# A late routing table moved to PSUM, and an order on ScalarE in a 128-row expert unit

## The chip, the cores and the metric

The kernel runs on one core of a Trainium2 chip. The metric is device time in microseconds (us) of one execution. The kernel before takes 699.88 us, the median of three runs (699.31 to 701.46). The profile is of another execution, which took 696.43 us.

## The reference

Inputs are q, k, v of shape (8 batches, 8 heads, 576 positions, 64). Two attentions are added: a local one, in which a position sees the positions at most 3 away, and a coarse one over means of 4 positions, repeated 4 times. The sum, as 4608 tokens of 512 values, goes into a mixture of 8 experts. Each token goes to one expert:

```
logits = x @ w_gate + modality_bias[modality_id]
e_idx = np.argmax(logits, axis=1)
gate_w = probs[np.arange(N), e_idx]           # softmax of the logits, at the chosen expert
...
h = np.maximum(x[mask] @ w1[e], 0.0)          # 512 -> 1024
out[mask] = gate_w[mask, None] * (h @ w2[e])  # 1024 -> 512
```

All is fp32. The kernel splits each fp32 operand of an expert's matmul into a high and a low part and makes three matmuls of one (high by high, high by low, low by high).

## The kernel before

**Stages.** For about the first 270 us the kernel computes attention, the router's logits and the places of the tokens. After that come the experts: 11 units of rows, one after another. A unit has up to 512 rows of one expert (H = 4 blocks of 128 rows). The order (line 1190) is: two early units of 4 blocks, six more units of 4 blocks ("p", pairs), and then the late units ("m"): one of 2 blocks, one of a single block of 128 rows, and one of 2 blocks. Behind them a loop (L1254) takes what is left; its count comes from the routing.

**Tables.** Which expert and which rows a unit has is worked out on VectorE (DVE) by `table` (L665): a prefix sum over experts, then for each unit a one-hot row (`oh`), and products and sums with it. Three large scratch arrays are used: `m`, `oh` and `o2`. `pairs` (L747) makes the table of the "p" units. `late` (L759) makes that of the "m" units and of the loop, from values that `pairs` leaves; `rest` (L776) makes the loop's list out of it. In both, the scratch has the tag "o" in the pool `xp`, three buffers of 128x512 fp32. The output tiles `o` of the units (L989) use the same three buffers, and so do the ReLU results of the 128-row unit (L954). An output tile is free when its scatter to memory (L998, an indirect DMA that GpSimd, POOL, issues) has landed. `C.ltri` is a 128x16x16 triangle of ones that `table` multiplies with in its first step. `pairs` is called before unit 0, `late` before unit 1.

**A unit.** `compute` (L921): the first layer makes groups of 128x512 in PSUM (L939; PSUM tag "S", three banks). ScalarE (ACT) takes the ReLU into `hh` (L943) and DVE the low part into `hl` (L944); then the bank is free. `second` (L972) makes the second layer (L987); ACT scales the result by the gate into `o` (L990), and POOL scatters it. The rows of the next unit are transposed on TensorE (PE) meanwhile (`xsplit`, L912; PSUM tag "T", three banks), and split by ACT (`xh`, L915) and DVE (`xl`, L917).

**The 128-row unit.** `compute_half` (L948) turns the roles round: the rows are stationary and the weights stream. So its result has to be transposed. For each half g of the 1024 hidden values: 12 matmuls (L961), ReLU on ACT into an `o` tile (L963), four transposes on PE into `ht` (L966, tag "T"), a copy on ACT into `hh` (L968), and a subtraction on DVE into `hl` (L969).

**Weights.** A unit has eight chunks of 128x1024 fp32: four of W1, four of W2. `step` (L1219) loads and splits the next chunk; it runs one unit ahead (LEAD = 8). Each chunk is a load into one of four `raw` buffers (L827 for W1, L829 for W2, issued on SyncE's queue SP), a copy on ACT into the high part `whi` (L848), and a subtraction on DVE into the low part `wlo` (L854). Where a chunk goes into the tile `X`, its parts are called `whl`. Within the 128-row unit, `compute_half` itself calls `step` four times (W1 of the last unit), and `second` four times (W2 of the last unit).

**Order.** From the experts on nothing is ordered by hand except by `issue_after(x)`: an instruction traced inside it comes behind x in the queue of its engine, without a semaphore. A scheduler orders the rest as the program is built, by readiness and program order. On the chip each of ACT, DVE, POOL and SP takes its instructions strictly in that order: one that waits holds up those behind it.

Of the kernel before, what the change touches and what calls it, by code (L numbers as in the profile page):

```python
# [7 lines left out]
F32 = mybir.dt.float32  # L8
F32R = mybir.dt.float32r
BF16 = mybir.dt.bfloat16  # L10
I32 = mybir.dt.int32
AF = mybir.ActivationFunctionType
# [6 lines left out]
NTOK, DM, NE, DF = 4608, 512, 8, 1024  # L19
# [23 lines left out]
NUMAX = NFULL + 1 + NLOOP  # L43
# [3 lines left out]
TB, SB = 3, 3  # L47
# [24 lines left out]
def whole(pieces):  # L72

    while True:
        try:
            next(pieces)
        except StopIteration as x:
            return x.value
# [417 lines left out]
class Router:  # L496
# [165 lines left out]
        s.nc.vector.tensor_copy(n, ni)  # L662
        yield

    def table(s, n, base, U, nm, pool, tag, unit=256):  # L665


        nc, C, tp = s.nc, s.C, s.tp
        N = n.shape[1]
        m = (pool.tile([128, DM], F32, name=tag, bufs=3)[:, : N * N].rearrange("p (a b) -> p a b", a=N) if tag else  # L670
             tp.tile([128, N, N], F32, name=nm + "m"))
        incl = tp.tile([128, N], F32, name=nm + "incl")
        nc.vector.tensor_tensor(m, C.ltri[:, :N, :N], n.unsqueeze(1).broadcast_to([128, N, N]), op=ALU.mult)
        yield
        nc.vector.tensor_reduce(incl, m, op=ALU.add, axis=AX.X)
        yield
        excl = tp.tile([128, N], F32, name=nm + "excl")
        nc.vector.tensor_tensor(excl, incl, n, op=ALU.subtract)
        yield

        off = tp.tile([128, N], F32, name=nm + "off")
        nc.vector.scalar_tensor_tensor(off, excl, -float(unit), base, op0=ALU.mult, op1=ALU.add)
        yield
        sh = [128, U, N]
        ub = C.uf[:, :U].unsqueeze(2).broadcast_to(sh)
        if tag:
            oh, o2 = (pool.tile([128, DM], F32, name=tag, bufs=3)[:, : U * N].rearrange("p (u l) -> p u l", l=N)
                      for _ in range(2))
        else:
            oh, o2 = (tp.tile(sh, F32, name=nm + x) for x in ("oh", "o2"))  # L690
        nc.vector.tensor_tensor(oh, incl.unsqueeze(1).broadcast_to(sh), ub, op=ALU.is_gt)
        yield
        nc.vector.tensor_tensor(o2, excl.unsqueeze(1).broadcast_to(sh), ub, op=ALU.is_gt)
        yield
        nc.vector.tensor_tensor(oh, oh, o2, op=ALU.subtract)
        yield
        r = tp.tile([128, 2, U], F32, name=nm + "r")
        for i, qv in enumerate((off, C.e2[:, :N])):
            nc.vector.tensor_tensor(o2, oh, qv.unsqueeze(1).broadcast_to(sh), op=ALU.mult)
            yield  # L700
            nc.vector.tensor_reduce(r[:, i], o2, op=ALU.add, axis=AX.X)
            yield
        nc.vector.scalar_tensor_tensor(r[:, 0], C.uf[:, :U], float(unit), r[:, 0], op0=ALU.mult, op1=ALU.add)
        yield

        no = tp.tile([128, U], F32, name=nm + "no")
        nc.vector.tensor_scalar(no, C.uf[:, :U], incl[:, N - 1 : N], float(NSLOT), op0=ALU.is_ge, op1=ALU.mult)
        yield
        nc.vector.tensor_tensor(r[:, 0], r[:, 0], no, op=ALU.add)
        yield  # L710
        return r, incl, excl
# [47 lines left out]
    def late(s, c, pool):  # L759

        nc, tp = s.nc, s.tp
        d = whole(s.taken(s.pn, s.pexcl, NPAIR, "p"))
        nc.vector.tensor_tensor(d, d, s.d, op=ALU.add)
        nc.vector.tensor_scalar(d, d, 2.0, None, op0=ALU.mult)
        n = tp.tile([128, 2 * NE], F32, name="mn")
        base = tp.tile([128, 2 * NE], F32, name="mbase")
        whole(s.units_of(c, 127, n[:, :NE], "m"))
        whole(s.units_of(c, 255, n[:, NE:], "mh"))
        nc.vector.tensor_tensor(n[:, NE:], n[:, NE:], n[:, :NE], op=ALU.subtract)
        for i, x in enumerate((d, n[:, :NE])):  # L770
            nc.vector.scalar_tensor_tensor(base[:, NE * i : NE * i + NE], x, 256.0, s.C.ecap, op0=ALU.mult, op1=ALU.add)
        nc.vector.tensor_tensor(n[:, :NE], n[:, :NE], d, op=ALU.subtract)
        s.r, s.incl, _ = whole(s.table(n, base, NUMAX, "m", pool, "o"))
        return whole(s.index(s.r, NFULL + 1, "m"))

    def rest(s):  # L776
# [16 lines left out]
class Moe:  # L793
    def __init__(s, tc, ctx, C, psum, xs, tab, w1, w2, out):
        s.tc, s.nc, s.C, s.ps = tc, tc.nc, C, psum
        s.xs, s.tab, s.w1, s.w2, s.out = xs, tab, w1, w2, out
        s.wr = ctx.enter_context(tc.tile_pool(name="mwr", bufs=4))
        s.wa = ctx.enter_context(tc.tile_pool(name="mwa", bufs=1))
        s.xa = ctx.enter_context(tc.tile_pool(name="mxa", bufs=1))
        s.na, s.ne = 2, 4  # L800
        s.turn = {}
        s.nw = 12
        s.cw, s.after = 0, ()

    def open_early(s, ctx):

# [26 lines left out]
    def wsplit(s, raw, which):  # L833
        nc = s.nc
        i = s.cw % s.nw
        turn = s.cw = s.cw + 1
        if i < s.nw - 2:
            pool = s.wa if i < s.na else s.we if i < s.na + s.ne else s.wb
            hi = pool.tile([128, 1024], F32R, name=f"whi{i}")
            lo = pool.tile([128, 1024], F32R, name=f"wlo{i}")  # L840
        else:
            X = s.xg.tile([128, 2560], F32R, name="whl", tag="X")
            hi, lo = X[:, :1024], X[:, 1024:2048]
        with ExitStack() as order:
            if HOLD <= turn <= NHOLD and s.after:
                for x in s.after:
                    order.enter_context(s.tc.issue_after(x.ins))
            (nc.gpsimd.tensor_copy if turn <= 4 else nc.scalar.copy)(hi, raw)  # L848
        yield
        with ExitStack() as order:  # L850
            if HOLD <= turn <= NHOLD and s.after:
                for x in s.after:
                    order.enter_context(s.tc.issue_after(x.ins))
            (nc.gpsimd if turn == 4 else nc.vector).tensor_tensor(lo, raw, hi.bitcast(F32), op=ALU.subtract)  # L854
        if which == 0:
            return hi, lo
        return hi.rearrange("p (f d) -> p f d", f=2), lo.rearrange("p (f d) -> p f d", f=2)
# [90 lines left out]
    def compute_half(s, T, W, X, step, mid, J):  # L948

        nc = s.nc  # L950
        xh, xl = X
        hh, hl = s.hidden()
        for g in range(2):
            r = s.xp.tile([128, 512], F32, name="o", bufs=3)  # L954
            p = s.ps.tile([128, 512], F32, name="l1", tag="S", bufs=SB)
            for k in range(4):
                if k % 2 == 0:
                    step()
                wh, wl = W[k]
                for i, (a, x) in enumerate(((xh, wh), (xl, wh), (xh, wl))):  # L960
                    nc.tensor.matmul(p, a[:, k, 0:128], x[:, 512 * g : 512 * g + 512], start=(k == 0 and i == 0),  # L961
                                     stop=(k == 3 and i == 2))
            nc.scalar.activation(r, p, AF.Relu)  # L963
            p = s.ps.tile([128, 4, 128], F32, name="ht", tag="T", bufs=TB)
            for f in range(4):
                nc.tensor.transpose(p[:, f, :], r[:, 128 * f : 128 * f + 128], s.C.ident)  # L966
            h4 = hh[:, 4 * g : 4 * g + 4, 0:128]
            nc.scalar.copy(h4, p)  # L968
            nc.vector.tensor_tensor(hl[:, 4 * g : 4 * g + 4, 0:128], p, h4.bitcast(F32), op=ALU.subtract)  # L969
        s.second(T, W, hh, hl, 1, step, mid, J)  # L970

    def second(s, T, W, hh, hl, H, step, mid, J=None, last=0):  # L972
# [34 lines left out]
def build(tc, q, k, v, mid, w_gate, bias, w1, w2, out):  # L1007
    nc = tc.nc
    with ExitStack() as ctx:
# [3 lines left out]
        ps = ctx.enter_context(tc.tile_pool(name="ps", bufs=2, space=PSUM))  # L1013
        xs = dp.tile([NTOK + 1, DM], F32, name="xs")
        tab = dp.tile([NSLOT + CAP, 2], I32, name="tab")
        C = Consts(tc, cp, ps)
        moe = Moe(tc, ctx, C, ps, xs, tab, w1, w2, out)
        with ExitStack() as actx:
            ectx = ExitStack()
            ro = Router(tc, ctx, C, ps, xs, tab, tables)  # L1020
# [14 lines left out]
            N = 4 * B  # L1035
# [195 lines left out]
        for i, (_, _, H) in enumerate(order):  # L1231
            if i == 0:
                with tc.high_priority():
                    lists["p"] = ro.pairs(cnt, moe.xp)
            if i == 1:
                lists["m"] = ro.late(cnt, moe.xp)
            if i:
                gather(i + 2)

            def mid(h):  # L1240
                if i == h == 0:
                    gather(2)
                split(i + 1, h)

            if H == 1:
                moe.compute_half(Ts[i], Ws[i], Xs[i], step, mid, Js.get(i))
            else:
                moe.compute(Ts[i], Ws[i], Xs[i], H, step, mid, Js.get(i), i == N - 1)
# [45 lines left out]
```

## Time and profile before

| | |
|---|---|
| time of the profiled execution | 696.43 us |
| its span | 694.7 us |
| busy, share of the span: PE / DVE / ACT / POOL | 94% / 57% / 52% / 40% |
| mean DMA rate over the span | 154 GB/s |
| weight copies on ACT, L848 into `whi` | 70 of 1051 ns |
| weight subtractions on DVE, L854 into `wlo` | 73 of 1223 ns |

A timeline row has the start in us from the span's start, the length in us, the engine, the line of the kernel, the operation, output <- input, their shapes, and the count of merged instructions. In brackets stand the idle time of the engine ahead of it, and what ended it, as semaphores let it be inferred. A row of the windows view has the window and its length, then the busy time and count of PE, of PE's weight loads (PEld), DVE, ACT and POOL, then the granted PE clock (PEclk, 1.00 is full speed), the DMA share, and GB/s. Matmuls overlap, so a matmul's length is more than the distance to the next one.

### The profile page before, as it was taken

To read this page: it belongs to the slowest core of one execution; us is meant where nothing else is said; L and a number is where in the kernel's file an instruction comes from. 1 tells how busy PE (TensorE), PEld (TensorE's weight loads), DVE (VectorE), ACT (ScalarE), POOL (GpSimd) and SP (SyncE) were. 2 spreads that over 40 slices of the span, in tenths; PEclk is the share of its full clock that TensorE was granted. 3 is DMA by queue.
4 is the path that set the end of the run, shared out by engine and by line. 5 is a ranking of instruction groups with operands and counts; after the bars stand their busy time and mean duration, and the time that the engine had idled before them with its cause. 6 is when DMAs were issued, how large, how long until landed. Compare 5 with 4: busy or idle time off the path is not lost. (4 is left out here: it accounts for less than half of the span.)

```text
span 694.7 us, 16603 instructions
## 1 busy us (share of the span) xinstructions
PE 650.9 (94%) x6123; PEld 514.1 (74%) x6123; DVE 393.9 (57%) x867; ACT 362.5 (52%) x804; POOL 280.2 (40%) x366
## 2 busy tenths in 40 slices
PE   7899989988989889998999999999999999999896
PEld 4566666665657567886888888888888888889694
DVE  6778778898887977647445234333453243416610
ACT  4788888875887645443344324333344244425610
POOL 5777676866788692361210400303104011210211
PEclk9999999998999999999999999999999999999999
DMA  9899879998599959296652544607434355245600
GB/s 189 170 181 175 164 164 200 174 172 175 113 202 172 165 153 247 61 320 210 170 194 70 148 147 123 239 9 201 158 97 139 98 145 174 65 134 181 203 29 30
DMA packets 176421, 106.97 MB, mean 154 GB/s; under 512 B 136300, under 2 KB 154770, under 8 KB 176338
## 3 DMA queue, kind: packets, MB, share of 16 engines
q1 hardware_dynamic: 169138, 86.71, 54.1%
q0 software_dynamic: 7200, 19.18, 8.4%
q8 instruction: 49, 0.80, 0.6%
q14 instruction: 34, 0.28, 0.2%
HBM read 86.61 MB, written 19.51 MB: 153 GB/s over the span
## 5 line engine op out<-in xcount | busy, mean ns | idle before, releaser
L998 POOL DMA_INDIRECT out_dram<-o,tg x34 | 36.9, 1085 | 249.0 <-ACT o L990 194.0
L854 DVE TENSOR_TENSOR wlo<-raw,whi 128x1024 fp32r<-128x1024 f32 x73 | 87.5, 1223 | 80.0 <-ACT whi L848 75.4
L944 DVE SCALAR_TENSOR_TENSOR hl<-l,hh 128x512 fp32r<-128x512 f32 x72 | 49.3, 688 | 103.6 <-ACT hh L943 103.6
L987 PE MATMUL l<-whi,hh 128*128 128x512 f32 x256 | 100.4, 396 | 3.1 <-ACT hh L968 3.1
L987 PE MATMUL l<-whi,hl 128*128 128x512 f32 x256 | 100.0, 391 | 0.0
L987 PE MATMUL l<-wlo,hh 128*128 128x512 f32 x256 | 100.0, 391 | 0.0
L943 ACT ACTIVATE hh<-l 128x512 fp32r<-128x512 f32 x72 | 42.6, 596 | 108.9 <-PE l L939 108.9
L939 PE MATMUL l<-xh,whi 128*128 128x512 f32 (+1 forms) x256 | 95.3, 375 | 3.3 <-DVE rcnt L789 1.7
L939 PE MATMUL l<-xl,whi 128*128 128x512 f32 (+1 forms) x256 | 94.9, 371 | 0.0
L939 PE MATMUL l<-xh,wlo 128*128 128x512 f32 (+1 forms) x256 | 94.8, 370 | 0.0
L848 ACT CAST whi<-raw 128x1024 fp32r<-128x1024 f32 x70 | 71.4, 1051 | 32.7 <-DMA raw<-in_moe_w_dram 20.3
L990 ACT ACTIVATE o<-l,tg 128x512 f32<-128x512 f32 x37 | 25.3, 687 | 98.9 <-PE l L987 70.9
L987 PEld LDWEIGHTS l<-whi,hh 128*128 128x128 f32 x256 | 48.3, 189 | 12.9 <-ACT hh L968 3.4
L939 PEld LDWEIGHTS l<-xh,whi 128*128 128x128 f32 x256 | 48.1, 189 | 12.9 <-DVE hl L944 2.1
L987 PEld LDWEIGHTS l<-wlo,hh 128*128 128x128 f32 x256 | 48.2, 188 | 10.1
L987 PEld LDWEIGHTS l<-whi,hl 128*128 128x128 f32 x256 | 48.4, 189 | 9.5
L939 PEld LDWEIGHTS l<-xh,wlo 128*128 128x128 f32 x256 | 48.3, 189 | 8.3
L939 PEld LDWEIGHTS l<-xl,whi 128*128 128x128 f32 x256 | 48.3, 189 | 8.0
L636 POOL DMA_INDIRECT tab<-ig,si x36 | 38.4, 1066 | 37.7 <-DVE si L607 16.3
L479 PE MATMUL avl<-Pw,vw 128*64 128x96 f32 x768 | 47.8, 263 | 1.0 <-ACT Od L469 0.5
L479 PEld LDWEIGHTS avl<-Pw,vw 128*64 128x64 f32 x768 | 35.9, 143 | 14.2 <-issue 6.8
L917 DVE TENSOR_TENSOR xl<-xt,xh 128x512 fp32r<-128x512 f32 x37 | 24.3, 681 | 37.8 <-ACT xh L915 37.7
(254 smaller groups left out, 1314.0 us busy)
## 6 DMA issues: line engine op xcount, KB each, us to landing
raw<-in_moe_w_dram SPq DMA_DIRECT2D x176, 128.0 KB
raw<-in_moe_w_dram SPq DMA_DIRECT2D x44, 512.0 KB
vw<-in_v_dram SPq DMA_DIRECT2D x53, 180.0 KB
qt<-in_q_dram SPq DMA_DIRECT2D x30, 288.0 KB
kt<-in_k_dram SPq DMA_DIRECT2D x30, 288.0 KB
xs<-R SPq DMA_DIRECT2D x64, 128.0 KB
vw<-in_v_dram SPq DMA_DIRECT2D x15, 90.0 KB
xs<-R SPq DMA_DIRECT2D x12, 64.0 KB
```

The lines of the kernel that those rows point to most:

```text
L479: s.nc.tensor.matmul(p[64 * a : 64 * a + 64, c], vw[:, NB * (4 * (hp // 2) + hp % 2 + 2 * a) + k, :], Pw[:, 2 * k + a], start=True, stop=T ...
L636: i = nc.gpsimd.indirect_dma_start(out=s.tab[:, :], out_offset=bass.IndirectOffsetOnAxis(ap=C.si[:, t : t + 1], axis=0), in_=C.ig[:, t, :] ...
L848: (nc.gpsimd.tensor_copy if turn <= 4 else nc.scalar.copy)(hi, raw)
L854: (nc.gpsimd if turn == 4 else nc.vector).tensor_tensor(lo, raw, hi.bitcast(F32), op=ALU.subtract)
L917: nc.vector.tensor_tensor(xl[:, :, hs], p, xh[:, :, hs].bitcast(F32), op=ALU.subtract)
L939: nc.tensor.matmul(p[:, f % n, :], a[:, fs], x[:, k, :N], start=(k == 0 and i == 0), stop=(k == 3 and i == 2))
L943: nc.scalar.activation(hh[:, g, :N], p, AF.Relu)
L944: nc.vector.scalar_tensor_tensor(hl[:, g, :N], p, 0.0, hh[:, g, :N].bitcast(F32), op0=ALU.max, op1=ALU.subtract)
L987: nc.tensor.matmul(p, a[:, f, hs], x[:, f % 2, :], start=(f == 0 and i == 0), stop=(f == 7 and i == 2))
L990: nc.scalar.mul(o, p, T[:, h, 1:2].bitcast(F32))
L998: nc.gpsimd.indirect_dma_start(out=s.out[:, :], out_offset=bass.IndirectOffsetOnAxis(ap=T[:, h, 0:1], axis=0), in_=o, in_offset=None, boun ...
```

## The change

There are two edits.

The first concerns `late`. Its table no longer takes its scratch from the "o" buffers. `m` and `o2` are taken from the PSUM tag "T", the ring of the transposes (its three banks, TB = 3, stay three). `oh`, which holds only zeros and ones, is written as bf16 over the memory of `C.ltri`, which no later table reads. The table of `pairs` stays in the "o" buffers.

The second concerns the 128-row unit. `compute_half` leaves a list behind its second half: nothing, that half's ReLU, that half's copy into `hh`, and the copy once more. The next four weight copies (the W2 chunks of the last unit) take one entry each, and come behind it on ACT's queue.

```
-    def table(s, n, base, U, nm, pool, tag, unit=256):
+    def table(s, n, base, U, nm, pool, tag, unit=256, last=0):
...
-        m = (pool.tile([128, DM], F32, name=tag, bufs=3)[:, : N * N].rearrange("p (a b) -> p a b", a=N) if tag else
+        m = (pool.tile([128, DM], F32, name=tag, bufs=TB)[:, : N * N].rearrange("p (a b) -> p a b", a=N) if tag else
...
-        if tag:
-            oh, o2 = (pool.tile([128, DM], F32, name=tag, bufs=3)[:, : U * N].rearrange("p (u l) -> p u l", l=N)
+        if last:
+            oh = C.ltri.bitcast(BF16).rearrange("p a b -> p (a b)")[:, : U * N].rearrange("p (u l) -> p u l", l=N)
+            o2 = pool.tile([128, DM], F32, name=tag, bufs=TB)[:, : U * N].rearrange("p (u l) -> p u l", l=N)
+        elif tag:
+            oh, o2 = (pool.tile([128, DM], F32, name=tag, bufs=TB)[:, : U * N].rearrange("p (u l) -> p u l", l=N)
...
-        s.r, s.incl, _ = whole(s.table(n, base, NUMAX, "m", pool, "o"))
+        s.r, s.incl, _ = whole(s.table(n, base, NUMAX, "m", pool, "T", last=1))
...
-        s.cw, s.after = 0, ()
+        s.cw, s.after, s.before = 0, (), []
...
+            x = s.before.pop(0) if s.before else None
+            if x is not None:
+                order.enter_context(s.tc.issue_after(x.ins))
             (nc.gpsimd.tensor_copy if turn <= 4 else nc.scalar.copy)(hi, raw)
...
-            nc.scalar.activation(r, p, AF.Relu)
+            relu = nc.scalar.activation(r, p, AF.Relu)
...
-            nc.scalar.copy(h4, p)
+            copy = nc.scalar.copy(h4, p)
...
+        s.before = [None, relu, copy, copy]
         s.second(T, W, hh, hl, 1, step, mid, J)
...
-                lists["m"] = ro.late(cnt, moe.xp)
+                lists["m"] = ro.late(cnt, ps)
```

## The prediction

> **What bounds the kernel now.** I read the busy shares first, then the waits of TensorE (PE), then the timelines of the engines around those waits.
>
> ```profile
> PE 650.9 (94%) x6123; PEld 514.1 (74%) x6123; DVE 393.9 (57%) x867; ACT 362.5 (52%) x804; POOL 280.2 (40%) x366
> ```
>
> PE is busy for 94% of the span, and no other engine comes near. So the question is where PE stands still in the part of the program that the change touches, the expert stage. The list of PE's waits from 270 us to the end (total us, times, longest) has three entries:
>
> ```profile
> PE l L987 <- ACT hh L968: 3.1, 1, 3.1
> PE l L939 <- DVE rcnt L789: 1.7, 1, 1.7
> PE l L939 <- DVE hl L944: 0.9, 1, 0.9
> ```
>
> The two edits stand beside these three: the first beside the table of the late units, which is on VectorE (DVE) when the 1.7 and 0.9 us arise; the second beside the unit of 128 rows, whose `hh` copy is the 3.1 us. Outside them PE has always work, so time taken out of them comes off the span, if nothing else is late next.
>
> **The 128-row unit, as it is.** Timelines of ScalarE (ACT) and of PE (start, length):
>
> ```profile
> 651.57 1.05 ACT L848 CAST whi<-raw 128x1024 fp32r<-128x1024 f32 x1 [0.34 <-DMA raw<-in_moe_w_dram]
> 652.85 1.04 ACT L848 CAST whi<-raw 128x1024 fp32r<-128x1024 f32 x1 [0.23 <-DMA raw<-in_moe_w_dram]
> 655.03 1.04 ACT L848 CAST whi<-raw 128x1024 fp32r<-128x1024 f32 x1 [1.14 <-SPq L1254]
> 655.98 0.58 ACT L968 CAST hh<-ht 128x512 fp32r<-128x512 f32 x1
> 656.46 0.60 ACT L963 ACTIVATE o<-l 128x512 f32<-128x512 f32 x1
> 656.95 1.05 ACT L848 CAST whi<-raw 128x1024 fp32r<-128x1024 f32 x1
> 658.19 0.59 ACT L968 CAST hh<-ht 128x512 fp32r<-128x512 f32 x1 [0.20 <-PE ht L966]
> ```
> ```profile
> 652.63 0.39 PE L961 MATMUL l<-wlo,xh 128*128 128x512 f32 x1
> 652.86 0.60 PE L966 MATMUL ht<-ident,o 128*128 128x128 f32 x4
> 656.61 0.50 PE L987 MATMUL l<-whi,hh 128*128 128x512 f32 x1 [3.15 <-ACT hh L968]
> 657.11 1.04 PE L966 MATMUL ht<-ident,o 128*128 128x128 f32 x4
> 657.95 1.92 PE L912 MATMUL xt<-ident,xg 128*128 128x128 f32 x8
> 659.51 0.78 PE L987 MATMUL l<-whi,hl 128*128 128x512 f32 x1
> 660.51 0.47 PE L987 MATMUL l<-whi,hh 128*128 128x512 f32 x1
> ```
>
> The first transposes `ht` end at 653.46 (652.86 + 0.60). Their copy L968 starts only at 655.98: between stand the second and third weight copies L848, and the third stood idle for 1.14 us first (by its place a late weight load; the name behind the arrow is a loop instruction at the program's end). ACT is in order, so the late load held back a copy that had nothing to do with it. The granted clock (column PEclk) shows a second loss behind the wait:
>
> ```profile
> 312.00:316.00 4.00, 2.34 (x12) 1.74 (x11) 3.50 (x11) 1.36 (x2) 1.48 (x1) 1.00 1.05 269
> 654.00:656.00 2.00, 0.00 (x0) 0.00 (x0) 1.15 (x1) 0.97 (x2) 1.00 (x1) 1.00 0.78 272
> 656.00:658.00 2.00, 1.39 (x6) 1.08 (x7) 1.83 (x2) 1.99 (x4) 0.01 (x1) 0.81 0.17 71
> 658.00:660.00 2.00, 2.00 (x10) 1.99 (x9) 1.98 (x3) 1.27 (x3) 1.79 (x1) 0.50 0.00 0
> ```
>
> After the 3.15 us wait PE runs at half clock around 658 to 660; after the 1.7 us wait near 313 the clock stayed at 1.00.
>
> **Part two of the change, the order on ACT.** It removes no instruction. The first W2 weight copy of the last unit keeps its freedom, the second is queued behind the second ReLU, the third and fourth behind the second `hh` copy. Step by step:
>
> - The first weight copy ends at 652.62 as now, before `ht` is there. The `hh` copy then starts 0.20 us after `ht`'s end, as its sister at 658.19 did: 653.66, and ends at 654.24. PE's first second-layer matmul starts 0.05 later, as at 656.61: 654.29.
> - The second ReLU overlaps the copy by 0.10 us (656.46 against 655.98 + 0.58): 654.14 to 654.74. I keep this order, since the ReLU's output tile can reuse the first one's only when `ht` is done. PE's second four transposes start at 654.80.
> - Four transposes take 0.35 us from start to start at full clock (next two rows), a 512-wide matmul 0.23 (652.63 to 652.86).
>
> ```profile
> 335.16 0.60 PE L912 MATMUL xt<-ident,xg 128*128 128x128 f32 x4
> 335.51 0.47 PE L987 MATMUL l<-whi,hh 128*128 128x512 f32 x1
> ```
>
> - So four `ht` and eight `xt` transposes run from 654.80 to 655.85, two more matmuls to 656.31. That is where PE stands today at 660.51. **Gain 4.2 us.** The cross-check by losses: PE is free at 653.23 and has 3 x 0.23 + 12 x 0.0875 = 1.74 us of work up to that point; today it takes 7.28, a loss of 5.54; then 3.08, a loss of 1.34.
>
> What is late next: the `hl` of the first half on DVE (0.68 us behind 654.24) is there at about 654.95, before PE asks at 655.85. The second weight copy lies ahead of the second `hh` copy and delays it to about 655.7; with 1.2 us for its own subtraction ahead of `hl` the second half is complete near 657.5, and PE asks for it after nine further matmuls, 656.31 + 2.07 = 658.4. The third and fourth weight copies move to about 656.2 to 658.3; behind them are at worst the two `xh` copies of the last unit, done with their subtractions by 660.5 where PE reaches that unit at about 661. Up to 0.6 us may be lost there, if PE's order asks sooner. The weights themselves have time: the last unit's last ReLU is at
>
> ```profile
> 677.11 0.60 ACT L943 ACTIVATE hh<-l 128x512 fp32r<-128x512 f32 x1 [2.28 <-PE l L939]
> ```
>
> and W2 is read only after the first layer. No weight load follows, so nothing on SP is queued behind the held copies. Bounds: below, the clock falls in spite of the shorter wait (rival two); above, PE puts the eight `xt` transposes, 0.70 us, into the remaining wait: 4.9.
>
> [...]
>
> **Part one, the late table.** Fourteen table instructions, two casts and eight for the loop's list stay on DVE; only their buffers change: two banks of the transposes' PSUM ring, and the triangle matrix, which nobody reads afterwards. Today, on DVE:
>
> ```profile
> 289.41 0.16 DVE L717 CAST pbi<-pr 128x6 int32<-128x6 f32 x1
> 298.75 1.23 DVE L854 TENSOR_TENSOR wlo<-raw,whi 128x1024 fp32r<-128x1024 f32 x1 [9.18 <-ACT whi L848]
> 310.55 0.43 DVE L673 TENSOR_TENSOR o<-ltri,mn 128x256 f32<-128x256 f32 x1 [6.40 <-DMA out_dram<-o,tg]
> 314.48 0.68 DVE L944 SCALAR_TENSOR_TENSOR hl<-l,hh 128x512 fp32r<-128x512 f32 x1
> 316.92 0.68 DVE L944 SCALAR_TENSOR_TENSOR hl<-l,hh 128x512 fp32r<-128x512 f32 x1
> 320.94 0.50 DVE L693 TENSOR_TENSOR o<-mexcl,uf 128x336 f32<-128x336 f32 x1
> 321.35 0.68 DVE L944 SCALAR_TENSOR_TENSOR hl<-l,hh 128x512 fp32r<-128x512 f32 x1
> ```
>
> The table waits 6.40 us for an output scatter to leave its buffer, with `hl` queued behind it. Without that wait it fits into the 9.18 us that DVE idles before 298.75: fourteen instructions of at most 0.50 us are 7.0. But does PE gain its 1.7 + 0.9? See what else `hl` waits for:
>
> ```profile
> 310.95 0.59 ACT L943 ACTIVATE hh<-l 128x512 fp32r<-128x512 f32 x1
> ...
> 314.64 1.05 ACT L848 CAST whi<-raw 128x1024 fp32r<-128x1024 f32 x1 [3.10 <-DMA raw<-in_moe_w_dram]
> 315.59 0.60 ACT L943 ACTIVATE hh<-l 128x512 fp32r<-128x512 f32 x1
> 318.71 1.05 ACT L848 CAST whi<-raw 128x1024 fp32r<-128x1024 f32 x1 [2.52 <-DMA raw<-in_moe_w_dram]
> 319.66 1.08 ACT L943 ACTIVATE hh<-l 128x512 fp32r<-128x512 f32 x2
> ```
> ```profile
> 315.21 0.51 PE L939 MATMUL l<-xh,whi 128*128 128x512 f32 x1 [1.66 <-DVE rcnt L789]
> 322.09 0.50 PE L939 MATMUL l<-xh,whi 128*128 128x512 f32 x1 [0.88 <-DVE hl L944]
> ```
>
> Each group of twelve matmuls (2.7 us) needs the bank of the third group before it, which is free when `hl` is done. The first `hl` follows its `hh` (311.54), at worst behind one weight subtraction of 1.23, and ends by 313.45; so the group at 315.21 starts at 313.55: 1.66 gained. The next needs the second `hl`, whose `hh` is at 315.59 behind a weight copy that waits for DMA; it ends at 317.60 as today, so PE waits there 1.3 us. The next needs the third, whose `hh` is at 319.66 behind the next late load; its `hl` loses only the 0.41 us of the table instruction ahead of it (320.94 to 321.35). So PE resumes at 321.68 for 322.09: **gain 0.4 us**; the wait goes over to the weight loads.
>
> Bounds. Above: 2.5, both waits whole, if ACT takes the ReLUs ahead of the late weight copies. Below: the DMA share in the 312 to 316 row is full, at 269 GB/s; the next weight load (0.52 MB) is issued sooner and, were it to overtake, would cost 1.9; but SP issues it behind these. The first table instruction ahead of the pair table's last cast would cost 0.43. PSUM banks held against a transpose: nought, since that ring has three and the table runs in DVE's idle time; five instructions of 0.50, 2.5 us, if it did not. I take 0.4, by the rows of the loads.
>
> **Sum.** The profiled execution took 696.43 us (span 694.7 and 1.7 around it), 3.45 below the median of the three runs, 699.88. 696.43 - 4.2 - 0.4 = 691.8; carried to the median, 695.3.
>
> **Rivals.**
>
> 1. *Slower: the late table gets ahead of the pair table.* SP waited for that table's result:
>
> ```profile
> SPq L816 <- DVE pbi L717: 10.0, 1, 10.0
> ```
>
> Behind this wait stand the weight loads that are late at 314.64 and 318.71, so each us added before 289.41 reaches PE whole. With all fourteen instructions ahead, 7.0 - 4.2 = 2.8 slower, 702.7; it decides the sign from 4.2 us on. Against it: the late table's input comes out of the pair table's prefix sums, so hardly more than one of its instructions can be ahead.
>
> 2. *The clock falls all the same.* Of today's loss of 5.54 us the wait is 3.38 (653.23 to 656.61) and the second ReLU's lateness 0.27; the other 1.9 is the clock's. If that stays, the gain is 4.2 + 0.4 - 1.9 = 2.7, 697.2. For it: PE still has two short waits, from 653.23 and from 654.52. Against: the two waits of 1.66 and 0.88 us left the clock at 1.00. [...]
>
> 3. *Both early waits go whole*, because ACT's order shifts: 4.2 + 2.5 = 6.7, 693.2. For it: the loads' copies and ReLUs are close together. Against: nothing in the change orders them.
>
> 4. *The order does not take.* Another copy or load stays ahead of the first `hh` copy: only part one, 699.5.
>
> **How the numbers follow.** Forecast 0.60; rivals 0.05, 0.13, 0.14, 0.08 in this order. A measurement of this kernel tells about 0.3%, 2.1 us, from no change. Faster: 0.60 + 0.14 + two thirds of rival two, 0.83. Same: rival four and the rest of two, 0.12. Slower: 0.05. The range reaches from 692.4 (rival three with the 4.9) to 698.6 (rival two with 1.4 lost in part one); outside lie rivals one and four.
>
> **What would show it.** Right: the first L968 about 0.2 us after the first `ht`, with only one of the four W2 copies L848 ahead of it; PE's wait there near 1.1 us; PEclk 1.00 throughout; the late L673 just behind L717 without a wait for a scatter; PE's waits at L939 near 1.3 and 1.2 us, released by `hl` behind weight loads. Wrong: a PE wait on a transpose's bank, the loads after 292 us issued later, a clock under 0.9 at the 128-row unit, or a new PE wait at the last unit's `xl` above 0.6 us.

## The result, and the profile after

The kernel after the change took 694.31 us (median of 20 runs, 689.38 to 702.26), the kernel before 698.5 us (20 runs beside them, 692.1 to 704.88). The ratio is 0.994, with a 95% interval from 0.9915 to 0.9964: 4.2 us faster (2.5 to 5.9), where 4.6 were forecast. The profiled execution of after has a span of 691.2 us, against 694.7. Lines move by six or seven: weight copy L848 is L854 in after, first-layer matmul L939 is L945, `hl` L944 is L950, the 128-row unit's ReLU L963, transposes L966 and copy L968 are L969, L972 and L974, second-layer matmul L987 is L994, output L990 is L997.

PE's waits from 270 us on, in after (total us, times, longest):

```profile
PE l L945 <- DVE hl L950: 3.4, 3, 2.1
PE l L994 <- ACT hh L974: 0.7, 1, 0.7
PE l L945 <- issue: 0.4, 1, 0.4
```

The 3.1 us wait for `hh` has become 0.7. The waits for `hl`, beside the late table, are longer than before (3.8 us with the one of issue, against 1.7 + 0.9). Both are looked at in turn.

**The 128-row unit.** ScalarE (ACT) and then PE, after:

```profile
651.72 1.05 ACT L854 CAST whi<-raw 128x1024 fp32r<-128x1024 f32 x1
653.87 0.59 ACT L974 CAST hh<-ht 128x512 fp32r<-128x512 f32 x1 [1.09 <-PE ht L972]
654.35 0.60 ACT L969 ACTIVATE o<-l 128x512 f32<-128x512 f32 x1
654.84 1.05 ACT L854 CAST whi<-raw 128x1024 fp32r<-128x1024 f32 x1
655.78 0.60 ACT L974 CAST hh<-ht 128x512 fp32r<-128x512 f32 x1
656.25 2.02 ACT L854 CAST whi<-raw 128x1024 fp32r<-128x1024 f32 x2
```
```profile
653.23 0.60 PE L972 MATMUL ht<-ident,o 128*128 128x128 f32 x4
654.51 0.51 PE L994 MATMUL l<-whi,hh 128*128 128x512 f32 x1 [0.68 <-ACT hh L974]
655.01 0.66 PE L972 MATMUL ht<-ident,o 128*128 128x128 f32 x4
655.50 1.04 PE L918 MATMUL xt<-ident,xg 128*128 128x128 f32 x8
656.83 0.39 PE L994 MATMUL l<-whi,hh 128*128 128x512 f32 x1
```

The order is as asked for: one free weight copy, then `hh`, ReLU, the second copy, the second `hh`, the last two copies. ACT now waits for PE (1.09 us) ahead of `hh`, instead of PE for ACT. From the start of the first `ht` transposes to the fourth second-layer matmul PE takes 656.83 - 653.23 = 3.60 us; before it took 660.51 - 652.86 = 7.65. Of the 4.05 us between them, 2.47 lie ahead of the first of these matmuls (1.28 from the transposes' start, before 3.75) and 1.58 behind it (2.32, before 3.90). The clock (the column before the last two), after:

```profile
654.00:656.00 2.00, 1.49 (x10) 1.18 (x11) 0.81 (x3) 2.00 (x4) 0.83 (x1) 1.00 0.97 332
656.00:658.00 2.00, 2.00 (x13) 1.70 (x12) 2.00 (x3) 2.00 (x3) 0.15 (x1) 1.00 0.19 74
658.00:660.00 2.00, 2.00 (x10) 1.68 (x9) 2.00 (x3) 1.25 (x3) 1.38 (x1) 1.00 0.00 0
```

It stays at 1.00 where before it was 0.81 and 0.50.

**The late table.** On VectorE (DVE), after:

```profile
290.25 0.16 DVE L720 CAST pbi<-pr 128x6 int32<-128x6 f32 x1
290.32 0.42 DVE L673 TENSOR_TENSOR T<-ltri,mn 128x256 f32<-128x256 f32 x1
292.04 0.51 DVE L696 TENSOR_TENSOR T<-mexcl,uf 128x336 f32<-128x336 f32 x1
295.39 0.17 DVE L720 CAST mbi<-mr 128x3 int32<-128x3 f32 x1
```

The table runs right behind the pair table and is through by 295.6, in time in which DVE stood idle before; the wait of 6.40 us for the scatter is gone. But see the second unit's first layer, ACT and PE:

```profile
315.43 1.05 ACT L854 CAST whi<-raw 128x1024 fp32r<-128x1024 f32 x1 [3.58 <-DMA raw<-in_moe_w_dram]
316.39 0.59 ACT L949 ACTIVATE hh<-l 128x512 fp32r<-128x512 f32 x1
```
```profile
313.27 0.50 PE L945 MATMUL l<-xh,whi 128*128 128x512 f32 x1 [0.92 <-DVE hl L950]
318.39 0.50 PE L945 MATMUL l<-xh,whi 128*128 128x512 f32 x1 [2.10 <-DVE hl L950]
321.91 0.50 PE L945 MATMUL l<-xh,whi 128*128 128x512 f32 x1 [0.38 <-DVE hl L950]
```

PE reaches the group at 313.27 where it reached it at 315.21 before, and loses the time again at 318.39: the weight copy at 315.43 has stood 3.58 us for its load, the ReLU is behind it, and `hl` behind the ReLU. PE resumes at 321.91, before at 322.09.

**The sum by stages.** Four starts cut the expert stage: the pair table's cast (`pbi`, L717 before and L720 after), the 17th and 32nd output `o` on ACT, and the last unit's first `o`. For after:

```profile
475.84 0.69 ACT L997 ACTIVATE o<-l,tg 128x512 f32<-128x512 f32 x1 [2.85 <-PE l L994]
...
627.66 0.68 ACT L997 ACTIVATE o<-l,tg 128x512 f32<-128x512 f32 x1
...
680.38 0.69 ACT L997 ACTIVATE o<-l,tg 128x512 f32<-128x512 f32 x1 [6.46 <-PE l L994]
```

and for before:

```profile
475.47 0.69 ACT L990 ACTIVATE o<-l,tg 128x512 f32<-128x512 f32 x1 [2.85 <-PE l L987]
...
627.29 0.68 ACT L990 ACTIVATE o<-l,tg 128x512 f32<-128x512 f32 x1
...
684.16 0.69 ACT L990 ACTIVATE o<-l,tg 128x512 f32<-128x512 f32 x1 [6.46 <-PE l L987]
```

From `pbi` to the 17th output (the table stage): 186.06 before, 185.59 after, 0.47 less. PE had entered the second unit about 1.5 us earlier in this execution of after (302.97 against 304.51), from the attention stage, which can only shorten it: the table's part is 0.47 at most. From there to the 32nd, the last of the units of 4 blocks: 151.82 in both. From there, over the 2-block unit and the 128-row unit, to the last unit's first output (the 128-row stage): 56.87 and 52.72, 4.15 less. Such differences inside one execution are much steadier than whole times, since the attention stage ahead of the experts varies by some us between executions: in the table below, which has the stages of every kernel, `pbi` comes between 286.63 and 294.84 us where nothing was put ahead of it, and the 128-row stage takes 52.72 or 52.73 in all with the order.

| kernel | `pbi` | 17th `o` | 32nd `o` | last unit's `o` | table stage | 128-row stage |
|---|---|---|---|---|---|---|
| before | 289.41 | 475.47 | 627.29 | 684.16 | 186.06 | 56.87 |
| after | 290.25 | 475.84 | 627.66 | 680.38 | 185.59 | 52.72 |
| table alone | 286.63 | 472.59 | 624.41 | 680.37 | 185.96 | 55.96 |
| order alone | 289.73 | 476.00 | 627.82 | 680.55 | 186.27 | 52.73 |
| before, 12 dummy matmuls | 286.88 | 472.93 | 624.75 | 679.60 | 186.05 | 54.85 |
| before, 4 dummy matmuls | 294.84 | 481.60 | 633.42 | 688.13 | 186.76 | 54.71 |
| after, ReLUs first | 290.85 | 473.99 | 625.81 | 678.53 | 183.14 | 52.72 |
| before, ReLUs first | 291.83 | 475.88 | 627.70 | 685.30 | 184.05 | 57.60 |
| order and ReLUs first, old table | 290.29 | 474.17 | 626.00 | 678.72 | 183.88 | 52.72 |
| after, loads earlier | 289.54 | 475.27 | 627.09 | 679.81 | 185.73 | 52.72 |
| after, ReLUs first, loads earlier | 294.22 | 474.45 | 626.27 | 678.99 | 180.23 | 52.72 |
| after, pair table late | 295.87 | 476.37 | 628.19 | 680.92 | 180.50 | 52.73 |

The table stage is comparable only where PE is equally far when `pbi` comes: in before, order alone, the three kernels with ReLUs first and without earlier loads, where the first expert output follows `pbi` by 0.3 to 0.4 us. In the last two rows `pbi` itself is late, so their 180 tells of that and not of the stage. In two of the kernels the clock was at half within this stage too: for 3.41 us from 312.32 in before with 12 dummy matmuls, behind a wait of 2.72 us, and for 6.83 us from 309.43 in after with loads earlier.

### The profile page after: what moved, and what is told of

Its sections match the earlier page's. It is cut to its first block, busy times and chain, and to the rows that moved or that the text cites. A ratio compares the mean times of both kernels' runs of the same rounds, so it can differ in the third digit from the quotient of the medians.

```text
span 691.2 us, 16601 instructions
## 1 busy us (share of the span) xinstructions
PE 649.1 (94%) x6123; PEld 510.8 (74%) x6123; DVE 394.4 (57%) x867; ACT 362.1 (52%) x804; POOL 281.0 (41%) x366
## 4 chain that ended last, share of the span: by engine, by line
PE 62%; DVE 11%; DMA 8%; issue 6%; SPq 5%; ACT 3%; POOL 3%; POOLq 0%; ACTq 0%; DVEq 0%
PE l L994 24%; PE l L945 22%; DMA raw<-in_moe_w_dram 3%; PE tp L288 3%; DMA xs<-R 3%; PE scd L388 2%; PE avl L479 2%; PE sc L363 2%; PE xt L918 2%; PE avd L464 2%; SPq L630 2%; DMA vw<-in_v_dram 1%; SPq L264 1%; DVE X L490 1%; SPq L830 1%
## 5 line engine op out<-in xcount | busy, mean ns | idle before, releaser
L950 DVE SCALAR_TENSOR_TENSOR hl<-l,hh 128x512 fp32r<-128x512 f32 x72 | 49.2, 688 | 103.2 <-ACT hh L949 103.2
L994 PE MATMUL l<-whi,hh 128*128 128x512 f32 x256 | 100.6, 397 | 0.7 <-ACT hh L974 0.7
L994 PE MATMUL l<-wlo,hh 128*128 128x512 f32 x256 | 99.7, 390 | 0.0
L994 PE MATMUL l<-whi,hl 128*128 128x512 f32 x256 | 99.6, 390 | 0.0
L945 PE MATMUL l<-xh,whi 128*128 128x512 f32 (+1 forms) x256 | 95.3, 375 | 4.0 <-DVE hl L950 3.6
L945 PE MATMUL l<-xl,whi 128*128 128x512 f32 (+1 forms) x256 | 94.8, 370 | 0.0
L945 PE MATMUL l<-xh,wlo 128*128 128x512 f32 (+1 forms) x256 | 94.7, 370 | 0.0
L854 ACT CAST whi<-raw 128x1024 fp32r<-128x1024 f32 x70 | 71.4, 1051 | 34.0 <-DMA raw<-in_moe_w_dram 22.4
L997 ACT ACTIVATE o<-l,tg 128x512 f32<-128x512 f32 x37 | 25.3, 687 | 93.3 <-PE l L994 56.3
L945 PEld LDWEIGHTS l<-xh,whi 128*128 128x128 f32 x256 | 48.1, 188 | 14.5 <-DVE hl L950 5.0
L994 PEld LDWEIGHTS l<-whi,hh 128*128 128x128 f32 x256 | 48.1, 188 | 10.5 <-ACT hh L974 0.9
L994 PEld LDWEIGHTS l<-wlo,hh 128*128 128x128 f32 x256 | 48.1, 188 | 10.2
L994 PEld LDWEIGHTS l<-whi,hl 128*128 128x128 f32 x256 | 48.1, 188 | 9.4
L945 PEld LDWEIGHTS l<-xh,wlo 128*128 128x128 f32 x256 | 48.3, 189 | 8.2
L945 PEld LDWEIGHTS l<-xl,whi 128*128 128x128 f32 x256 | 48.3, 189 | 7.9
L479 PE MATMUL avl<-Pw,vw 128*64 128x96 f32 x768 | 46.2, 256 | 1.6 <-issue 1.0
L479 PEld LDWEIGHTS avl<-Pw,vw 128*64 128x64 f32 x768 | 34.3, 137 | 14.7 <-issue 9.7
```

The costliest lines, as they stand in the source:

```text
L479: s.nc.tensor.matmul(p[64 * a : 64 * a + 64, c], vw[:, NB * (4 * (hp // 2) + hp % 2 + 2 * a) + k, :], Pw[:, 2 * k + a], start=True, stop=T ...
L945: nc.tensor.matmul(p[:, f % n, :], a[:, fs], x[:, k, :N], start=(k == 0 and i == 0), stop=(k == 3 and i == 2))
L950: nc.vector.scalar_tensor_tensor(hl[:, g, :N], p, 0.0, hh[:, g, :N].bitcast(F32), op0=ALU.max, op1=ALU.subtract)
L994: nc.tensor.matmul(p, a[:, f, hs], x[:, f % 2, :], start=(f == 0 and i == 0), stop=(f == 7 and i == 2))
L997: nc.scalar.mul(o, p, T[:, h, 1:2].bitcast(F32))
```

## The experiments

The theory (A) was that of the prediction: the order in the 128-row unit brings nearly everything, a good part of it through the clock; the table's own wait is replaced by late weight loads. The first rival (B) gave the table a good part of the gain, since its wait of 6.40 us is gone; further rivals stand with the runs that test them. Each time is a ratio to the kernel before, run on the same chip.

**1. The table alone.** The change without its order:

```diff
-        s.before = [None, relu, copy, copy]
```

> The table in PSUM alone, without the order in the 128-row unit. Theory A (the late weight loads take over the wait): 0.4 us less than before, ratio 0.999; PE still waits about 2 us or more in all at the first layer of the second unit, released by hl behind late weight copies; the 3.1 us at the first hh copy of the 128-row unit and the half clock behind it stay. Rival B (the scatter wait was the cause, and both PE waits go whole): 2.5 us less, ratio 0.996.

Measured: 1.0018 (0.9986 to 1.005), 694.78 us against 693.83. No gain that can be told; a gain above 1.0 us is excluded, and with it the rival. The table stage is 185.96, 0.10 less than before. The 128-row unit has its old order (a late load, then `hh`), on ACT:

```profile
651.48 1.04 ACT L854 CAST whi<-raw 128x1024 fp32r<-128x1024 f32 x1 [1.15 <-SPq L1260]
652.43 0.58 ACT L974 CAST hh<-ht 128x512 fp32r<-128x512 f32 x1
```

**2. The order alone.** The change with the old table (its scratch in the output ring again):

```diff
-        s.r, s.incl, _ = whole(s.table(n, base, NUMAX, "m", pool, "T", last=1))
+        s.r, s.incl, _ = whole(s.table(n, base, NUMAX, "m", pool, "o"))
...
-                lists["m"] = ro.late(cnt, ps)
+                lists["m"] = ro.late(cnt, moe.xp)
```

> The order in the 128-row unit alone, the table in its old buffers. Theory A: 4.1 us less than before, ratio 0.994, the first hh copy within 0.3 us of the first ht transposes, clock 1.00 through the unit; the table's 6.4 us wait for a scatter stays. Rival B (this part has the rest of the measured 4.2 us after the table's 2.5): 1.7 us less, ratio 0.9975.

Measured: 0.9972 (0.9939 to 1.0004), 692.32 us. The interval holds what both theories say, so the timing decides nothing. The trace does: the 128-row stage is 52.73, 4.14 less than before, although the table waits as it did, 7.36 us:

```profile
311.40 0.43 DVE L673 TENSOR_TENSOR o<-ltri,mn 128x256 f32<-128x256 f32 x1 [7.36 <-DMA out_dram<-o,tg]
```

**3. The clock by itself.** Before, with twelve matmuls on a tile of zeros (added work whose result nobody reads) put into PE's wait, behind the first `ht`; the `hh` copy stays behind the late weight copy (`ht` in the code is the last of the first four transposes):

```diff
...
+        with s.tc.issue_after(ht.ins):
+            s.C.busy(nc, 12)
         s.second(T, W, hh, hl, 1, step, mid, J)
```

> The kernel before, with twelve matmuls of zeros behind the first ht transposes of the 128-row unit, in PE's wait; nothing else moved. Theory A (the wait costs a second time through the clock): the first hh copy is as late as before, but the clock stays at 1.00, the work behind runs at full speed, and the time is 1.9 us less, ratio 0.9973. Rival C (what follows the wait was slow because it waited for ACT and DVE, not by the clock): no change, ratio 1.000, or a little slower by the added matmuls.

Measured: 0.9964 (0.9931 to 0.9996), 692.4 us; the 128-row stage is 54.85, 2.02 less than before. PE, the `hh` copy on ACT, and then the row of the clock behind the wait:

```profile
650.32 0.60 PE L966 MATMUL ht<-ident,o 128*128 128x128 f32 x4
650.76 2.75 PE L129 MATMUL bz<-dummy 128*128 128x512 bf16 x12
653.72 0.50 PE L991 MATMUL l<-whi,hh 128*128 128x512 f32 x1 [0.21 <-ACT hh L970]
```
```profile
653.09 0.58 ACT L970 CAST hh<-ht 128x512 fp32r<-128x512 f32 x1
```
```profile
654.00:656.00 2.00, 2.00 (x15) 1.72 (x15) 1.91 (x3) 2.00 (x5) 0.03 (x1) 1.00 0.18 70
```

The `hh` copy is nearly as late as before (2.77 us behind the transposes' start, before 3.12), so 0.35 of the 2.02 us come from `hh` in this execution and not from the clock. The clock stays at 1.00, and from the first second-layer matmul to the fourth PE takes 2.33 us, as in after (2.32), where it took 3.90 before. So the clock's part is 1.6 to 1.7 us; 1.7 is also half of the 3.42 us that before ran at half clock (657.23 to 660.65, last section). A second version with four dummy matmuls asks how little work keeps the clock:

> The kernel before with four matmuls of zeros instead of twelve behind the first ht transposes, so that PE's wait there falls from some 3 us to about 2 us but is not filled. Theory A (a wait of 1.7 to 2.4 us leaves the clock alone, one of 2.5 or more halves it): clock 1.00 behind the wait, and the stage from the last output of the 2-block unit before it to the last unit's first output takes about 54.9 us as with twelve. Rival C (any idle time ahead of the unit counts): the clock falls, 56 us or more.

Measured (one run, 700.81 us; its attention stage was about 5 us later than that of before, which says nothing of the edit): the stage is 54.71, PE still waits 1.76 us, and the clock stays. (The stage is the one of the table; it starts at the last output of the units of 4 blocks, not of the 2-block unit.) PE, then the row of the clock:

```profile
662.21 0.51 PE L991 MATMUL l<-whi,hh 128*128 128x512 f32 x1 [1.76 <-ACT hh L970]
```
```profile
662.00:664.00 2.00, 1.79 (x13) 1.45 (x14) 1.91 (x3) 2.00 (x5) 0.01 (x1) 1.00 0.18 70
```

Here `hh` came 0.5 us earlier than in before (3.22 us from the transposes' start to that matmul), so this stage too has some 1.6 us from the clock. That four suffice is shown for this execution alone. The two bounds of theory A agree with most waits of the traces up to then (1.66 and 2.43 us with 1.00 behind them, 2.48, 2.72, 2.91 and 3.15 us with half clock); they are an estimate from such waits and do not hold in general. In this same execution a wait of 1.88 us, which ended at 272.33, was followed by half clock (272.76 to 276.17), and one of 2.48 us in the order alone was not (267.31; the table of the last section has all of them).

**4. The ReLUs ahead of the late weight copies.** If late loads on the in-order ACT are what took the table's gain, an order for the second unit's first layer as well should bring it:

```diff
...
             if step and f % 2 == 0 and 0 in ks:
+                if H == 4 and s.turn["h"] == 1 and f:
+                    s.before = [relu[{2: 0, 4: 3, 6: 5}[f]]]
                 step()
...
-                nc.scalar.activation(hh[:, g, :N], p, AF.Relu)
+                relu.append(nc.scalar.activation(hh[:, g, :N], p, AF.Relu))
```

> The changed kernel, and in the second unit's first layer the second, third and fourth W1 copies queued on ACT behind the first, fourth and sixth ReLU, so that no ReLU stands behind a late load. Theory A: the PE waits there (3.8 us in the changed kernel's profile, 2.5 in the one of before) go, so 2.5 to 3.8 us less than the changed kernel, 6.7 to 8 less than before, ratio 0.990. Rival D (lateness of the loads comes out elsewhere: later copies, later loads behind them, a wait in the next unit): as the changed kernel, ratio 0.994.

Measured: 0.9887 (0.9839 to 0.9935), 688.07 us. The table stage is 183.14, 2.45 less than in after. ACT and PE's waits from 262 us on:

```profile
311.92 0.60 ACT L951 ACTIVATE hh<-l 128x512 fp32r<-128x512 f32 x1
314.66 0.60 ACT L951 ACTIVATE hh<-l 128x512 fp32r<-128x512 f32 x1 [2.13 <-PE l L947]
317.39 0.60 ACT L951 ACTIVATE hh<-l 128x512 fp32r<-128x512 f32 x1 [2.13 <-PE l L947]
317.88 1.04 ACT L854 CAST whi<-raw 128x1024 fp32r<-128x1024 f32 x1
```
```profile
PE l L947 <- DVE hl L952: 2.4, 1, 2.4
PE l L996 <- ACT hh L976: 0.7, 1, 0.7
```

Now the ReLUs wait for PE and the weight copies stand behind them; PE has no wait left in the second unit (the 2.4 us is in the first, at 268.42). It has the lowest ratio of this study. Its interval still touches that of after against before, so that it beats after rests on the stages of the traces.

**5. The same order with the old table**, to see which of the two is the cause: before plus the diff of 4, and nothing in the 128-row unit.

> The kernel before (old table, no order in the 128-row unit) with the ReLUs of the second unit's first layer ahead of the late weight copies, as in the run before. Theory A (two causes side by side: the table's scatter waits on DVE, and the late loads on ACT, each enough for most of PE's waits): little gain, 0 to 0.9 us against before, measured from the pair table's last cast to the next units in the trace, where the same order together with the new table gave 2.9; ratio 0.999. Rival E (the late loads alone were the cause): 2.5 us, ratio 0.9965.

Measured: 1.0004 (0.9968 to 1.0041), no difference in the timing. In the trace the table stage is 184.05, 2.0 less than before. Theory A's expectation for the stage failed: I had taken the table's wait for the pace-setter in before. The table still waits for its buffer, nearly as long as before, but PE's wait behind it is 0.53 us and not 1.66 (DVE, PE):

```profile
312.09 0.43 DVE L673 TENSOR_TENSOR o<-ltri,mn 128x256 f32<-128x256 f32 x1 [5.99 <-DMA out_dram<-o,tg]
```
```profile
316.03 0.50 PE L947 MATMUL l<-xh,whi 128*128 128x512 f32 x1 [0.53 <-DVE rei L726]
```

In before the first `hl` stands on DVE behind the table and two weight subtractions (311.35 and 313.27) and starts 25.07 us behind `pbi`. Here it stands behind the table and one (312.88) and starts 23.47 us behind it: the second subtraction went back with its copy. So the larger cause is ACT's order; the table's buffer comes second. In this execution the 128-row stage was 57.60, as the clock was at half there for 6.83 us (655.94 to 662.77), twice as long as in before; whether that was so in the other executions, too, is not known. So I corrected theory A, and ran the combination that was still missing:

**6. The order in both units with the old table.**

> Both orders on ACT (the changed kernel's in the 128-row unit, and the ReLUs of the second unit's first layer ahead of the late weight copies), with the table in its old buffers. Theory A, corrected (the late loads on ACT are the larger cause, the table's scatter wait the smaller): about 0.9 us more than with the new table, 4.2 + 2 = 6.2 us less than before, ratio 0.991; some PE wait under 1 us stays at the second unit's first layer, released by DVE. Rival H (with the ReLUs in front the table's wait takes over fully, 1.7 to 2.5 us): 4.5 to 5 us less than before, ratio 0.993 to 0.9935, and a PE wait of 1.7 us or more.

Measured: 0.9948 (0.9914 to 0.9983). The table stage is 183.88, against 183.14 with the new table: the table's buffers are worth about 0.7 us once ACT's order no longer hides them (0.9 by the kernel of 5; single executions both). PE's waits in the second unit come to 0.2 us, so the rival with a wait of 1.7 us or more is out. The timing interval separates neither.

**7. Loads earlier.** After, with the third unit's gather traced two steps later, so that more weight loads are issued ahead of it:

```diff
-                if i == h == 0:
+                if i == 0 and h == 2:
```

> The changed kernel with the third unit's gather traced two row blocks later, so that two of the second unit's W2 loads stand ahead of SyncE's wait for the pair table. Theory A (the loads behind that wait are late): the four W1 loads behind come some 3 us earlier against the pair table's last cast, and the PE waits of the second unit's first layer shrink by 1 to 3 us; ratio to before 0.990 to 0.993. Rival F: the gather's later rows make PE wait at a transpose instead; ratio 0.994 or more.

Measured: 0.9983 (0.995 to 1.0017), 694.11 us. A miss for both theories. The four W1 copies came 2.0, 0.7, 1.4 and 1.7 us earlier against `pbi` than in after, not some 3. And the scheduler put one more of them ahead of the first unit's last output, which PE's next group waits for, and ahead of the first ReLU; PE waited in one piece (ACT, PE):

```profile
308.94 1.04 ACT L854 CAST whi<-raw 128x1024 fp32r<-128x1024 f32 x1 [3.06 <-DMA raw<-in_moe_w_dram]
309.89 0.68 ACT L997 ACTIVATE o<-l,tg 128x512 f32<-128x512 f32 x1
```
```profile
310.62 0.79 PE L945 MATMUL l<-xh,whi 128*128 128x512 f32 x1 [3.72 <-ACT o L997]
```

From 309.43 to 316.26 the clock was at half besides, so the wait was paid for a second time.

With ACT's order of experiment 4 besides:

> The changed kernel with the ReLUs of the second unit's first layer ahead of the late weight copies, and two W2 loads ahead of the wait for the pair table. Theory A: with the order of the ReLUs the late loads cost nothing any more, so the earlier loads add nothing, ratio 0.989 as with the order alone. Rival F: the later gather costs, ratio 0.992 or more.

Measured: 0.9914 (0.988 to 0.9947), 691.07 us: no more than the ReLU order by itself. From PE's entry into the second unit to the 17th output it takes 167.92 us (306.53 to 474.45), with the ReLU order alone 167.96 (306.03 to 473.99). When the order on ACT is right, earlier loads add nothing that can be measured.

**8. The pair table late.** Rival one of the prediction gave each us ahead of the pair table its full price. After, with seven chained DVE instructions (a delay that leaves the data as they are) ahead of it:

```diff
-        whole(s.units_of(c, 127, n, "p", 9))
+        w = pool.tile([128, DM], F32, name="o", bufs=TB).rearrange("p (a b) -> p a b", b=NE)
+        nc.vector.tensor_copy(w, c.unsqueeze(1).broadcast_to([128, 64, NE]))
+        for _ in range(6):
+            nc.vector.tensor_tensor(w, w, c.unsqueeze(1).broadcast_to([128, 64, NE]), op=ALU.max)
+        whole(s.units_of(w[:, 0], 127, n, "p", 9))
```

> The changed kernel with seven more DVE instructions of 128x512 chained ahead of the pair table, which do nothing but delay it, by about 3 us. Theory A (the loads behind the pair table set this stage): the delay reaches the following units whole, about 3 us, ratio to before 0.998. Rival G (PE sets this stage and has slack): under 1 us of it arrives, ratio 0.994 to 0.995.

Measured: 0.9971 (0.9942 to 0.9999), 693.41 us; after's own ratio is 0.994. The cast `pbi` came at 295.87, 5.62 us later than in after. The loads moved with it: the four W1 copies start 17.96, 20.90, 24.90 and 29.39 us behind `pbi`, in before 17.72, 20.59, 25.23 and 29.30. The 17th output came only 0.53 us later than in after, so little of the delay arrived there. But it is not a clean test: PE entered the second unit 2.1 us later than in after, too (305.05), and the scheduler's order on ACT changed, so that two ReLUs now stand ahead of a late copy (ACT).

```profile
311.94 1.07 ACT L953 ACTIVATE hh<-l 128x512 fp32r<-128x512 f32 x2
313.83 1.05 ACT L858 CAST whi<-raw 128x1024 fp32r<-128x1024 f32 x1 [0.81 <-DMA raw<-in_moe_w_dram]
```

So the premise of rival one is borne out, that the loads follow the pair table; its price is not confirmed, and what a delay costs with after's order on ACT stays open.

## Why the prediction was right

- **Part two, 4.2 us.** The 128-row stage gave 4.15, and the row-to-row sum 4.05. All six other kernels with the order have 52.72 or 52.73; those without it and without dummies 55.96, 56.87 and 57.60. Steps: the `hh` copy started 0.04 us after `ht`'s end (653.83) and not 0.20 after. PE's wait was 0.68 us; the 1.1 of the prediction counts from where PE is free (653.23), and counted as the profile counts it, from `ht`'s end at 653.46, its working gives 0.83. The second weight copy went ahead of the second `hh` as forecast. No loss arose at the last unit: no wait is listed there.
- **The clock, put at 1.9 us of it.** That it costs a part of its own is shown by the dummy matmuls. Its size was a little less: 1.6 to 1.7 us. The prediction took as the clock's all that was left of today's loss, and its sum had the twelve transposes at 1.05 us; in after they take 1.28 at full clock (655.01 to 656.29). The rest, some 2.5 us, is the earlier `hh` copy. The sum also had full clock behind the shortened wait: before shows that behind waits of 1.66 and 0.88 us, after behind this one of 0.68 us (654 to 660).
- **Part one, 0.4 us.** The table stage gave at most 0.47 in after and 0.10 with the table alone; the timing of the table alone cannot tell 0.4 from nothing. So 0.47 beside a forecast of 0.4 is no confirmation of the size. That the wait goes over to the weight loads is shown by experiment 4: with the ReLUs ahead of those loads it disappears. Mis-sized was its split: I had waits of 1.3 and 1.2 us, found were 0.92, 2.10 and 0.38, because PE entered the unit earlier and the loads did not (the late copies start 25.18 and 28.70 us behind `pbi`, before 25.23 and 29.30). And one reading of before was wrong, though the sum did not rest on it: the table's wait looked like the cause of 1.66 us, but with ACT's order put right and the old wait in place most of that goes as well (experiment 5).
- **Rivals.** Two (the clock falls all the same): out, 1.00 in the trace of after from 242 us to the last matmul; its 2.7 us lie within the interval of the timing. Three (both early waits go whole): out in after; it takes the order of experiment 4, which was not in the change. Four: out. One: the table did not get ahead of the pair table (290.32 against 290.25); its price stays open (experiment 8).
- **What stays open.** Whole times of this kernel spread by 1 to 2% between executions, so no timing here separates the order's 4.1 us from 2, or 0.7 us of the table from nothing. Those rest on stage differences of single profiled executions, which agree to 0.01 us where the 128-row order is the same.

## What to carry to other kernels

Look whether the instruction that PE waits for stands, on its engine, behind a copy that waits for a transfer, and whether it could go ahead: on ACT the `hh` copy, whose input was there at 653.46, started at 655.98 behind a weight copy that had stood idle for 1.14 us; put ahead of it, it started 0.04 us after its input. A wait that disappears beside a second one of the same stage brings only the difference: 6.40 us of DVE's waiting were worth 0.5 us at most, as the next engine's loads were late too. And price a PE wait of some us with the clock behind it: here the 3.15 us wait cost 1.6 to 1.7 us more after it had ended.

## What the runs showed of the hardware

**Instructions behind one that waits.** Four waits of before, and what stood behind each. ACT stood 1.14 us for the weight copy at 655.03, with the `hh` copy behind it (655.98) ready since 653.46. DVE stood 6.40 us for the table's buffer until 310.55; the weight subtraction behind it (311.35) had its `whi` at 308.18. POOL stood 4.71 us for a gather's rows until 296.38; behind that gather and three more, the scatter of the output tile that was there at 294.03 started at 302.88. SP stood 10.0 us for `pbi`, and in experiment 8, with `pbi` 5.62 us later than in after, the copies of the loads behind it came as long after `pbi` as before, to within 0.4 us.

**The clock behind a wait.** Short stretches in before (PEclk is the third number from the end):

```profile
657.20:657.60 0.40, 0.40 (x3) 0.40 (x4) 0.40 (x2) 0.40 (x1) 0.00 (x0) 0.54 0.00 0
...
660.60:661.00 0.40, 0.40 (x3) 0.35 (x2) 0.40 (x1) 0.00 (x0) 0.00 (x0) 0.94 0.79 328
```

and with the table alone:

```profile
653.00:653.40 0.40, 0.33 (x1) 0.29 (x1) 0.40 (x1) 0.40 (x2) 0.00 (x0) 0.59 0.64 266
...
656.40:656.80 0.40, 0.40 (x3) 0.33 (x2) 0.40 (x1) 0.34 (x1) 0.16 (x1) 0.89 0.00 0
```

A mean of 0.54 over 0.40 us is half clock for 0.37 of it. So before runs at half clock from 657.23 to 660.65, and the table alone from 653.07 to 656.49: 3.42 us both times, though PE had resumed 0.62 us before the first and at the same moment as the second.

Some of PE's waits from 260 us on, with the clock behind them:

| wait, us | kernel | PE resumes at | clock |
|---|---|---|---|
| 1.66 | before | 315.21 | 1.00 |
| 1.76 | before, 4 dummy matmuls | 662.21 | 1.00 |
| 1.88 | before, 4 dummy matmuls | 272.33 | half, 272.76 to 276.17 |
| 2.10 | after | 318.39 | 1.00 |
| 2.1 | order alone | 316.06 | 1.00 |
| 2.43 | after, ReLUs first | 268.42 | 1.00 |
| 2.48 | order alone | 267.31 | 1.00 |
| 2.48 | table alone | 653.07 | half, 653.07 to 656.49 |
| 2.72 | before, 12 dummy matmuls | 312.28 | half for 3.41 us from 312.32 |
| 2.91 | before, ReLUs first | 656.79 | half, 655.94 to 662.77 |
| 3.15 | before | 656.61 | half, 657.23 to 660.65 |
| 3.72 | after, loads earlier | 310.62 | half, 309.43 to 316.26 |

The length of a wait alone does not tell in these executions: two of 2.48 us ended differently, and 1.88 us lost the clock in the execution in which 1.76 us kept it. In two of the rows the half clock began while PE still waited. The four of 2.72 us and more were all followed by half clock; what decides for the shorter ones is not shown.

All three profiles with the old order and no dummy matmuls lost the clock in the 128-row unit, behind waits of 3.15, 2.48 and 2.91 us (before, the table alone, before with ReLUs first). Their 128-row stages of 56.87, 55.96 and 57.60 put the order's gain at 3.2 to 4.9 us, by execution. Where the clock stays it would be about 2.5, an estimate: the 4.15 of before and after, less the 1.6 to 1.7 of experiment 3. How often it stays, and so what the gain is over many executions, is not measured.
